# Moving the output bias into accumulating DMAs, and three halving adds for a reduction, in a fused attention and MLP kernel

## The chip, the cores and the metric

The kernel runs on one core of a Trainium2 chip. The metric is the device time of one execution in microseconds (us), taken as the median of several executions. The kernel before takes 215.47 us (three executions, 214.64 to 215.5). The profile is one of these executions; its span, from the first instruction to the last, is 212.9 us.

The engines are named as the profile names them: PE is TensorE (matmuls), PEld its weight loads, DVE is VectorE, ACT is ScalarE, POOL is GpSimd, SP is SyncE, which here only issues DMAs.

## What is computed

A layer norm of x feeds two branches, and both are added to x. With S = 2048 rows of D = 640:

```python
xn = layernorm(x)                          # rows of 640
q, k, v = split(xn @ wqkv)                 # 32 heads of 20
# row s attends to the 8 rows s, s-2, ..., s-14; rows before 0 get -1e9
logits[h, s, w] = (q[h, s] . k[h, s - 2*w]) * 20**-0.5
attn = softmax(logits, axis=w)
o[h, s] = sum_w attn[h, s, w] * v[h, s - 2*w]
out = x + o @ wo + (gelu(xn @ w1 + b1) @ w2 + b2)      # w1: 640 x 1536
```

All inputs and the output are bfloat16.

## The kernel before

The rows are worked in four chunks of 512 (`CH`), each with four blocks of 128. A small list scheduler inside the program fixes the order of instructions on PE, DVE, ACT and SP: each piece has an engine, an estimated duration, a rank, the pieces it needs and the buffers it holds. A table of rank offsets (`RANK`) tunes that order. The engines then run their instructions in this fixed order and wait on semaphores. POOL is outside of this order.

The pieces that matter here, for chunk n:

```python
# buffers: name, how many
("acc", 4), ("L", 1), ("O", 1), ("xnT", 3), ..., ("prod", 4),
("e", 1), ("attn", 1), ("ax", 1), ("oT", 1), ("hT", 18), ("osb", 2), ...

def do_ld():                                  # SP, after the transposes of chunk 1
    nc.sync.dma_start(w2_sb[:], ...)
    nc.sync.dma_start(wo2[:], ...)
    nc.sync.dma_start(b2bc[:], b2_bcast)      # b2 on all 128 partitions

def do_xb(n):                                 # DVE: x + b2, then stored to the output rows
    cs = slice(n * BPC, (n + 1) * BPC)
    nc.vector.tensor_tensor(out=x_sb[:, cs, :], in0=x_sb[:, cs, :],
        in1=b2bc[:].unsqueeze(1).to_broadcast([P, BPC, D]), op=ALU.add)
    cs = slice(n * BPC, min((n + 1) * BPC, LASTB))
    nc.sync.dma_start(out_sd.rearrange("(b p) d -> p b d", p=P)[:, cs, :], x_sb[:, cs, :])

def do_qk(n, wp, i):                          # DVE: q * shifted k, 128 x 2560 (two per wp)
    nc.vector.tensor_tensor(out=prod[:, i, :, :], in0=q, in1=k[:, :, off : off + CH], op=ALU.mult)

def logits(L, prod, wp):                      # PE: sums over a head's channels, into PSUM tile L
    for t in range(KT):
        for j in range(BPC):
            nc.tensor.matmul(L[j * H : (j + 1) * H, 2 * wp : 2 * wp + 2, :], lhsT=head_of[:],
                             rhs=prod[:, :, t, j * P : (j + 1) * P], ...)

# softmax over the 8 positions w, tile [128, 8, 128]
def do_mask():                                # chunk 0 only, DVE on PSUM
    nc.vector.tensor_tensor(out=L[0:H, :, 0:MW], in0=L[0:H, :, 0:MW], in1=mask[:], op=ALU.add)
def do_max(n): nc.vector.tensor_reduce(...)   # m over w
def do_sub(n): nc.vector.tensor_tensor(...)   # z = L - m
def do_exp(n): nc.scalar.activation(e[:], tiles["z", n][:], ACT.Exp, scale=SCALE)
def do_sum(n):
    nc.vector.tensor_reduce(out=ssum[:], in_=e.rearrange("p w c -> p c w"), axis=AX.X, op=ALU.add)
def do_recip(n): nc.vector.reciprocal(rs[:], tiles["ss", n][:])
def do_attn(n): nc.vector.tensor_tensor(...)  # e * rs

# attn is broadcast to the channels of each head by DMA (SP and ACT queues) into ax,
# DVE multiplies shifted v with it (do_av, 8 per chunk, 128 x 2560 each), adds the eight
# in pairs (do_add, do_add, do_add, then do_ot, which writes oT)

def do_f1(n, ft): ...                         # PE: 5 matmuls of 512 columns -> hps (PSUM, "acc")
def do_ge(n, ft): ...                         # ACT: gelu -> hT
def do_pj(n, which, to): ...                  # PE: 5 matmuls of 512 columns -> pps; chunks 1 to 3
                                              # (chunk 0 uses 128 columns each: gps)
def do_o(n, bl, pc, parts):                   # PE: one output block, 5 parts: 12 pairs from hT, w2
    ...                                       # and 5 pairs from oT, wo (the last part)
    nc.tensor.matmul(lo[:], lhsT=lhs, rhs=rhs[:, 0:CH], ...)
    nc.tensor.matmul(hi[:, 0 : D - CH], lhsT=lhs, rhs=rhs[:, CH:D], ...)
def do_oc(n, bl):                             # ACT: PSUM -> osb
    nc.scalar.copy(osb[:, 0:CH], lo); nc.scalar.copy(osb[:, CH:D], hi)
def do_od(n, bl):                             # POOL's queue: osb is added to the output rows
    nc.gpsimd.dma_start(rows, osb[:], accum_op=ALU.add)
```

For chunks 0 to 2 each output block uses one pair of PSUM tiles (`lo`, `hi`, the buffer "O"), so a block can start only when ACT has copied the block before it out. The last block of all is not accumulated by DMA: VectorE adds `x_sb` to its PSUM tiles and stores them (`do_oclo`, `do_ochi`).

Of the kernel before, what the change touches and what calls it, by code (L numbers as in the profile page):

```python
# [11 lines left out]
ALU = mybir.AluOpType  # L12
AX = mybir.AxisListType
BF16 = mybir.dt.bfloat16
F32 = mybir.dt.float32
PE, VE, SE, DQ = "pe", "ve", "se", "dq"


class Plan:
# [101 lines left out]
S, D, F, H, W, DIL = 2048, 640, 1536, 32, 8, 2  # L121
P = 128
# [3 lines left out]
CH = 512  # L126
NCH = S // CH
BPC = CH // P
# [3 lines left out]
MASKED = -1e9  # L132
MW = 16
LASTB = S // P - 1
# [4 lines left out]


RANK = {
    "ad02": 77, "av2": -4.2, "f11": 11.8, "f12": 26.1, "ge0": 15.4, "gj1": -111.8, "gj2": -25.5, "o00": -38,
    "o10": 29.1, "o11": 22.3, "o12": 28, "o13": 9.4, "o20": 9.6, "o21": 2.7, "o22": -7.9, "pj11": -100.5,
    "qk3": -49.5, "rc1": -43.4, "rc3": -86.1, "st2": 49.8, "st3": 51.7, "xn2": 23.8,
}


def make_plan(fns, offsets=RANK):

    pl = Plan(offsets)  # L150
# [6 lines left out]
    def f(kind, *a):  # L157
        return lambda: fns[kind](*a)
# [6 lines left out]
    for n in range(NCH):  # L165
        base = n * PERIOD
        prev = base - PERIOD
        early = base + (-37.0 if n == 1 else -85.0)
        xnT, q, k, v, oT = (("xnT", n), ("q", n), ("k", n), ("v", n), ("oT", n))
# [11 lines left out]
        for bl in range(BPC):  # L181
            xn, tp = ("xn", n, bl), ("acc", "tp", n, bl)
# [5 lines left out]
            pl.add(f"tc{n}{bl}", SE, 0.65, early + -3.0 if n else -99, [f"tp{n}{bl}"], f("tc", n, bl), [tp, xnT])  # L188
        if n == 1:
            pl.add("ld", DQ, 9.2, -1000, [f"tc1{bl}" for bl in range(BPC)], f("ld"))  # L190
        pl.add(f"xb{n}", VE, 1.43, base + 36, [f"xn{n}{bl}" for bl in range(BPC)] + ["ld"], f("xb", n))

        if n == 0:
            for bl in range(BPC):
                for g, parts in enumerate(GROUPS):
                    ps, last = ("acc", "g", bl, g), max(p[0] for p in parts)
# [5 lines left out]
        for which, buf in enumerate((q, k, v)):  # L202
# [5 lines left out]
            if which:  # L208
                need = done(n - 1, which) if n else []
                bufs = [buf] + ([("k" if which == 1 else "v", n - 1)] if n else [])  # L210
                pl.add(f"pad{n}{which}", SE, 0.26, early if n else -50, need, f("pad", n, which), bufs)

        L = ("L", n)
        for wp in range(W // 2):
            pr = ("prod", "qk", n, wp)
            for i in range(2):
                need = done(n, 0) + done(n, 1) + [f"pad{n}1"]
                pl.add(f"qk{n}{wp}{i}", VE, 1.42, base + 3.0 * wp + i, need, f("qk", n, wp, i), [q, k, pr])
            group = 2 if n else 4
            if wp % group == group - 1:  # L220
                wps = range(wp - group + 1, wp + 1)
                need = [f"qk{n}{x}{i}" for x in wps for i in range(2)] + ([f"lg{n}{wp-group}"] if wp > group else [])
                every = [("prod", "qk", n, x) for x in wps]
                pl.add(f"lg{n}{wp}", PE, 0.16 + 0.52 * group, n - 1000, need, f("lg", n, wps), every + [L], slack=0.8)

        e, at, ax = ("e", n), ("attn", n), ("ax", n)
        m, rs, ss, z = ("m", n), ("rs", n), ("ss", n), ("prod", "z", n)
        if n == 0:
            pl.add("mk", VE, 0.26, n - 1000, ["lg03"], f("mask"), [L])
        pl.add(f"m{n}", VE, 1.22, n - 1000, [f"lg{n}3"] + ([] if n else ["mk"]), f("max", n), [L, m])  # L230
        pl.add(f"mx{n}", VE, 1.22, n - 1000, [f"m{n}"], f("sub", n), [L, m, z])
        pl.add(f"ex{n}", SE, 1.02, n - 1000, [f"mx{n}"], f("exp", n), [z, e], table="exp")
        pl.add(f"ss{n}", VE, 1.93, n - 1000, [f"ex{n}"], f("sum", n), [e, ss])
        pl.add(f"ri{n}", VE, 0.96, n - 1000, [f"ss{n}"], f("recip", n), [ss, rs])
        pl.add(f"at{n}", VE, 1.22, n - 1000, [f"ri{n}"], f("attn", n), [e, rs, at])
        pl.add(f"xs{n}", SE, 1.2, n - 1000, [f"at{n}"], f("xs", n), [at, ax])
# [3 lines left out]
        for wp in range(W // 2):  # L240
            for i in range(2):
                need = [f"xd{n}", f"xs{n}", f"pad{n}2"] + done(n, 2)
                pl.add(f"av{n}{wp}{i}", VE, 1.42, base + 15.0 + 6.0 * wp + i, need, f("av", n, wp, i), [v, ax, prs[wp]])
        for k2, (a, b, r) in enumerate(((0, 1, 9.0), (2, 3, 21.0), (0, 2, 22.0))):
            need = [f"av{n}{x}{i}" for x in (a, b) for i in range(2)] if k2 < 2 else [f"ad{n}0", f"ad{n}1"]
# [8 lines left out]
        for bl in range(BPC):  # L254
            ob = ("osb", n, bl)
            O = [("O", n, bl)] if n < NCH - 1 or bl % 2 == 0 else [("acc", "lo", n, bl), ("acc", "hi", n, bl)]
            final = n * BPC + bl == LASTB
            last = None
            for pc in range(5):
                need = [last] if last else [f"ge{n}{ft}" for ft in range(FT)] + [f"xb{n}", "ld"]  # L260
                if pc == 4:
                    need.append(f"ot{n}")
                us = (0.65, 0.65, 0.65, 0.65, 1.08)[pc] if final else (0.82, 0.82, 0.82, 0.82, 1.37)[pc]
                last = pl.add(f"o{n}{bl}{pc}", PE, us, base + PERIOD + 8.0 + 8.0 * bl, need, f("o", n, bl, pc, ("lo",) if final else ("lo", "hi")), O + (hTs if pc == 0 else hTs[3 * pc : 3 * pc + 3] if pc < 4 else [oT]))
            if final:
                pl.add("oclo", VE, 0.65, base, [last], f("oclo"), O + [ob])
                last = pl.add("ohi", PE, 1.05, base + PERIOD + 90, [last], f("ohi"), O)
                pl.add("ochi", VE, 0.25, base, [last], f("ochi"), O + [ob])
                continue
            pl.add(f"oc{n}{bl}", SE, 0.78, base, [last], f("oc", n, bl), O + [ob])  # L270
            pl.add(f"od{n}{bl}", SE, 0.0, base, [f"oc{n}{bl}"], f("od", n, bl), [ob])
# [4 lines left out]
def kernel(  # L276
# [16 lines left out]
    nc = tc.nc  # L293
# [3 lines left out]
    out_sd = out.rearrange("b s d -> (b s) d")  # L297
    x_nb = x_sd.rearrange("(b p) d -> p b d", p=P)

    consts = ctx.enter_context(tc.tile_pool(name="consts", bufs=1))  # L300
# [8 lines left out]
    smp = ctx.enter_context(tc.tile_pool(name="smp", bufs=1))  # L309
# [6 lines left out]
    x_sb = wts.tile([P, NCH * BPC, D], BF16, name="x_sb")  # L316
# [3 lines left out]
    wo2 = wts.tile([P, KT, D], BF16, name="wo2")  # L320
    b1_rt = consts.tile([P, P], BF16, name="b1_rt")
    b2bc = consts.tile([P, D], BF16, name="b2bc")
    wqkv_v = A_wqkv.rearrange("(t p) n -> p t n", p=P)
    b2_bcast = bass.AP(tensor=B_b2.tensor, offset=B_b2.offset, ap=[[0, P], [1, D]])
    nc.sync.dma_start(x_sb[:, 0, :], x_nb[:, 0, :])
# [6 lines left out]
    for n in range(1, NCH):  # L332
        cs = slice(n * BPC, (n + 1) * BPC)
# [13 lines left out]
    nc.gpsimd.memset(eps_t[:], EPS)  # L347
    warm = consts.tile([P, 1], F32, name="warm")
    nc.scalar.activation(warm[:], eps_t[:], ACT.Sqrt)
    mask = consts.tile([H, W, MW], F32, name="mask")  # L350
    nc.gpsimd.memset(mask[:], 0.0)
    for w in range(1, W):
        nc.gpsimd.memset(mask[:, w, 0 : DIL * w], MASKED)
    head_of = consts.tile([P, H], BF16, name="head_of")
    b1T = consts.tile([P, FT], F32, name="b1T")

# [75 lines left out]
            tiles["tp", n, bl][:, 0 : KT * P].rearrange("p (t m) -> p t m", t=KT),  # L432
        )


    def do_td(n, bl):
        xnT = get(("xnT", n), lambda: xtp.tile([P, KT, CH], BF16, tag="xnT", name="xnT"))
        nc.sync.dma_start_transpose(xnT[:, :, bl * P : (bl + 1) * P], tiles["xn", n, bl][:])

    def do_xb(n):  # L440
        cs = slice(n * BPC, (n + 1) * BPC)
        nc.vector.tensor_tensor(
            out=x_sb[:, cs, :],
            in0=x_sb[:, cs, :],
            in1=b2bc[:].unsqueeze(1).to_broadcast([P, BPC, D]),
            op=ALU.add,
        )
        cs = slice(n * BPC, min((n + 1) * BPC, LASTB))
        nc.sync.dma_start(out_sd.rearrange("(b p) d -> p b d", p=P)[:, cs, :], x_sb[:, cs, :])


    def qkv_tile(n, which):
# [66 lines left out]
            op=ALU.mult,  # L519
        )  # L520

    def do_lg(n, wps):
        L = get(("L", n), lambda: psL.tile([P, W, P], F32, tag="L", name="L"))
        for wp in wps:
            logits(L, tiles["qk", n, wp], wp)

    def do_mask():
        L = tiles["L", 0]
        nc.vector.tensor_tensor(out=L[0:H, :, 0:MW], in0=L[0:H, :, 0:MW], in1=mask[:], op=ALU.add)

    def logits(L, prod, wp):
        for t in range(KT):
            for j in range(BPC):
                nc.tensor.matmul(  # L534
                    L[j * H : (j + 1) * H, 2 * wp : 2 * wp + 2, :],
                    lhsT=head_of[:],
                    rhs=prod[:, :, t, j * P : (j + 1) * P],
                    start=(t == 0 and wp % 2 == 0),
                    stop=(t == KT - 1 and wp % 2 == 1),
                    skip_group_check=True,  # L540
                )
# [22 lines left out]
        nc.scalar.activation(e[:], tiles["z", n][:], ACT.Exp, scale=SCALE)  # L564

    def do_sum(n):
        ssum = smp.tile([P, P], F32, tag="ssum", name="ssum")
        tiles["ss", n] = ssum
        nc.vector.tensor_reduce(
            out=ssum[:], in_=tiles["e", n][:].rearrange("p w c -> p c w"), axis=AX.X, op=ALU.add  # L570
        )

    def do_recip(n):
        rs = smp.tile([P, P], F32, tag="rs", name="rs")
        tiles["rs", n] = rs
        nc.vector.reciprocal(rs[:], tiles["ss", n][:])

    def do_attn(n):
        attn = smp.tile([P, W, P], BF16, tag="attn", name="attn")
# [98 lines left out]
    def do_oclo():  # L678
        osb = outp.tile([P, D], BF16, tag="osb", name="osb")
        tiles["osb", last] = osb  # L680
        nc.vector.tensor_tensor(out=osb[:, 0:CH], in0=tiles["lo", *last][:], in1=x_sb[:, LASTB, 0:CH], op=ALU.add)  # L681
        nc.sync.dma_start(out_sd[LASTB * P :, 0:CH], osb[:, 0:CH])

    def do_ohi():
# [3 lines left out]
    def do_ochi():  # L688
        osb = tiles["osb", last]
        nc.vector.tensor_tensor(  # L690
            out=osb[:, CH:D], in0=tiles["hi", *last][:, 0 : D - CH], in1=x_sb[:, LASTB, CH:D], op=ALU.add
        )
        nc.scalar.dma_start(out_sd[LASTB * P :, CH:D], osb[:, CH:D])

# [39 lines left out]
```

## Time and profile before

| what | value |
|---|---|
| time, median of three | 215.47 us |
| span of the profiled execution | 212.9 us |
| PE busy | 206.3 us |
| DVE busy | 181.0 us |
| ACT busy | 106.9 us |
| POOL busy | 14.4 us |
| bias additions on DVE (L442, 128 x 2560) | 4 of 1485 ns |
| reductions for the sum on DVE (L569) | 4 of 1909 ns |
| mask addition on DVE (L529) | 1 of 287 ns |
| output stores on POOL (L673) | 15, median 3.4 us from issue to landing |
| x stores on SP (L449) | 4, 2.7 to 8.0 us from issue to landing |
| broadcasts ax<-attn | 16 issues of 256 KB, median some 6 us to landing |

The busy share of an engine counts its instructions only, and matmuls overlap one another, so a busy PE is read together with its list of waits. A row in the list of groups gives line, engine, operation, output and inputs with shapes, the count, the busy time, the mean duration in ns of one, and the idle time of the engine just ahead of it. The slices divide the span into 40 stretches of 5.3 us, and each digit is a busy share in tenths.

### The profile page before, as it was taken

The page shows a single profiled execution, that of the slowest core. Times are in us where ns is not written, and L with a number is a line of the kernel's source. Part 1 is how long each engine was busy: PE and PEld are TensorE (multiplying, and loading weights), DVE is VectorE, ACT ScalarE, POOL GpSimd, SP SyncE. Part 2 cuts the span into 40 slices and gives each one's busy share as a digit, 9 for nine tenths or more (in the row PEclk, how much of TensorE's full clock was granted, in tenths as well). Part 3 has the DMA queues.
Part 4 walks back from the last instruction along what each step waited for, and adds up shares of the span by engine and source line. Part 5 has one row for each costly group of instructions (what it writes and reads, how often), then busy time and mean ns, then how long its engine had stood idle before and what let it go on. Part 6 is the DMA issues. An engine that isn't in the chain of part 4 may idle for free.

```text
span 212.9 us, 3938 instructions
## 1 busy us (share of the span) xinstructions
PE 206.3 (97%) x1667; PEld 121.4 (57%) x1690; DVE 181.0 (85%) x171; ACT 106.9 (50%) x190; POOL 14.4 (7%) x32
## 2 busy tenths in 40 slices
PE   7899999999999999999999999999999999999994
PEld 7799845644644556556555555556454555555552
DVE  3849899699999999997999999999999869995001
ACT  3667895798469664725346462243565311351210
POOL 2000000000000000110001100110101011101220
PEclk9999999999999999999999999999999999999999
DMA  6999539556711210227002080220205912152223
GB/s 217 366 367 370 83 68 329 217 167 172 199 31 31 56 39 0 31 34 197 0 3 31 4 211 17 31 29 5 32 3 83 259 20 30 24 123 31 34 31 63
DMA packets 21449, 21.49 MB, mean 101 GB/s; under 512 B 9016, under 2 KB 18616, under 8 KB 21432
## 3 DMA queue, kind: packets, MB, share of 16 engines
q1 hardware_dynamic: 17832, 16.49, 25.9%
q0 software_dynamic: 2160, 2.46, 9.5%
q10 hardware_dynamic: 1440, 2.29, 4.5%
q8 instruction: 13, 0.21, 0.4%
q14 instruction: 4, 0.03, 0.1%
HBM read 10.00 MB, written 5.08 MB: 71 GB/s over the span
## 4 chain that ended last, share of the span: by engine, by line
PE 95%; DMA 1%; DVE 1%; issue 1%; ACT 0%
PE lo L660 27%; PE hps L629 24%; PE pps L465 23%; PE gps L482 8%; PE hi L662 8%; PE L L534 4%; DMA x_sb<-in_A_x_dram 1%; PE tp L426 0%; DVE stats L385 0%; DVE stats L386 0%; ACT xnT L430 0%; DVE xn L412 0%; DVE mv L387 0%; DVE osb L690 0%; PE b_tp L366 0%
## 5 line engine op out<-in xcount | busy, mean ns | idle before, releaser
L629 PE MATMUL hps<-xnT,w_sb 128*128 128x512 bf16 x235 | 54.1, 379 | 0.3
L660 PE MATMUL lo<-w_sb,hT 128*128 128x512 bf16 x185 | 52.2, 379 | 0.0
L607 DVE TENSOR_TENSOR pv<-vT,ax 128x2560 bf16<-128x2560 bf16 x32 | 46.0, 1485 | 3.8 <-DMA ax<-attn 3.8
L515 DVE TENSOR_TENSOR prod<-qT,kT 128x2560 bf16<-128x2560 bf16 x32 | 45.5, 1483 | 0.0
L662 PE MATMUL hi<-w_sb,hT 128*128 128x128 bf16 x192 | 40.3, 219 | 0.6 <-issue 0.3
L640 ACT ACTIVATE hT<-hps,b1T 128x512 bf16<-128x512 f32 x48 | 31.3, 687 | 16.8 <-PE hps L629 12.2
L629 PEld LDWEIGHTS <-w_sb 128*128 128x128 bf16 x240 | 22.9, 98 | 26.8 <-issue 0.3
L616 DVE TENSOR_TENSOR pv<-pv 128x5120 bf16<-128x5120 bf16 x12 | 33.9, 2824 | 0.3
L667 ACT CAST osb<-lo 128x512 bf16<-128x512 f32 x15 | 8.8, 585 | 45.8 <-PE hi L662 21.6
L660 PEld LDWEIGHTS <-hT 128*128 128x128 bf16 x192 | 18.7, 98 | 22.6 <-issue 0.4
L673 POOL DMA_DIRECT2D out_dram<-osb x15 | 13.1, 875 | 192.4 <-ACT osb L668 192.4
L660 PE MATMUL lo<-wo,oT 128*128 128x512 bf16 x76 | 22.3, 379 | 0.1
L662 PEld LDWEIGHTS <-hT 128*128 128x128 bf16 x192 | 18.4, 98 | 1.8
L465 PE MATMUL pps<-xnT,wk_sb 128*128 128x512 bf16 x72 | 16.9, 380 | 0.2
L662 PE MATMUL hi<-wo,oT 128*128 128x128 bf16 x80 | 16.9, 219 | 0.2
L465 PE MATMUL pps<-xnT,wv_sb 128*128 128x512 bf16 x73 | 16.8, 379 | 0.2 <-issue 0.2
L465 PE MATMUL pps<-xnT,wq_sb 128*128 128x512 bf16 x73 | 16.8, 379 | 0.1
L660 PEld LDWEIGHTS <-oT 128*128 128x128 bf16 x80 | 7.8, 98 | 9.4
L681 DVE TENSOR_TENSOR osb<-lo,x_sb 128x512 bf16<-128x512 f32 x1 | 0.7, 691 | 14.5 <-PE lo L660 14.5
L385 DVE BATCH_NORM_STATS2 stats<-x_sb 128x6 f32<-128x320 bf16 x16 | 7.3, 459 | 6.7 <-DMA x_sb<-in_A_x_dram 6.5
L500 ACT CAST kT<-pps 128x512 bf16<-128x512 f32 x15 | 8.8, 584 | 8.2 <-PE pps L465 8.2
L465 PEld LDWEIGHTS <-wk_sb 128*128 128x128 bf16 x75 | 8.6, 118 | 7.4 <-issue 0.4
(61 smaller groups left out, 211.5 us busy)
## 6 DMA issues: line engine op xcount, KB each, us to landing
w_sb<-in_B_w_dram SPq DMA_DIRECT2D x2, 1920.0 KB, 11.6
out_dram<-osb POOLq DMA_DIRECT2D x15, 160.0 KB, 3.4
ax<-attn SPq DMA_DIRECT2D x8, 256.0 KB, 6.0
ax<-attn ACTq DMA_DIRECT2D x8, 256.0 KB, 5.5
x_sb<-in_A_x_dram SPq DMA_DIRECT2D x3, 640.0 KB, 11.4
out_dram<-x_sb SPq DMA_DIRECT2D x3, 640.0 KB, 3.7
wq_sb<-in_A_wqkv_dram SPq DMA_DIRECT2D x1, 800.0 KB, 4.8
wk_sb<-in_A_wqkv_dram SPq DMA_DIRECT2D x1, 800.0 KB, 7.0
```

Of the source, the lines that this page charges most:

```text
L465: nc.tensor.matmul(ps[:], lhsT=wqkv_p[which][:, ti, to, :], rhs=xnT[:, ti, :], start=(ti == 0), stop=(ti == KT - 1),)
L482: nc.tensor.matmul(ps[:, i, :], lhsT=wqkv_p[which][:, ti, to, :], rhs=tiles["xnT", 0][:, ti, cs], start=(ti == 0), stop=(ti == KT - 1),)
L500: nc.scalar.copy(dest[:, to, off : off + CH], tiles["pps", n, which, to][:])
L515: nc.vector.tensor_tensor(out=prod[:, i, :, :], in0=qkv_tile(n, 0)[:], in1=qkv_tile(n, 1)[:, :, off : off + CH], op=ALU.mult,)
L607: nc.vector.tensor_tensor(out=pv[:, i, :, :].rearrange("p t (j c) -> p t j c", j=BPC), in0=qkv_tile(n, 2)[:, :, off : off + CH].rearrange( ...
L616: nc.vector.tensor_tensor(out=ta[:], in0=ta[:], in1=tb[:], op=ALU.add)
L629: nc.tensor.matmul(ps[:], lhsT=w1_sb[:, ti, ft * P : (ft + 1) * P], rhs=tiles["xnT", n][:, ti, :], start=(ti == 0), stop=(ti == KT - 1),)
L640: nc.scalar.activation(hT[:], tiles["hps", n, ft][:], ACT.Gelu_apprx_tanh, bias=b1T[:, ft : ft + 1], scale=1.0)
L660: nc.tensor.matmul(lo[:], lhsT=lhs, rhs=rhs[:, 0:CH], start=first, stop=last)
L662: nc.tensor.matmul(hi[:, 0 : D - CH], lhsT=lhs, rhs=rhs[:, CH:D], start=first, stop=last)
L667: nc.scalar.copy(osb[:, 0:CH], tiles["lo", n, bl][:])
L673: nc.gpsimd.dma_start(rows, tiles["osb", n, bl][:], accum_op=ALU.add)
```

## The change

Four things are changed together.

1. The output rows first get x by a plain DMA (`do_xp`, SP), and then the bias b2, from its tile that holds it on all partitions, by an accumulating DMA (`do_xb`, POOL's queue). VectorE no longer adds the bias to x, except for the last block (`do_xl`), which does not go through accumulating DMAs. This frees VectorE and takes the dependence of the x store on VectorE away.
2. The exponentials are summed in three halving adds (8 to 4, 4 to 2, 2 to 1 positions) instead of one strided reduction.
3. The first chunk's logits are made in two groups of 40 matmuls, as those of the other chunks were already, instead of one group of 80. The mask for the first 14 rows is added by a matmul of one partition into PSUM after each group, instead of by VectorE.
4. The rank offsets are new, so that pieces stand in another order on all engines. POOL's four bias DMAs stand ahead of all 15 output stores.

The diff, cut to its core:

```diff
 RANK = {
-    "ad02": 77, "av2": -4.2, "f11": 11.8, ...
+    "ad00": 78, "av0": 30, "av1": 231.2, "av2": 188.6, "f10": 41.2, ...
 }
-        pl.add(f"xb{n}", VE, 1.43, base + 36, [f"xn{n}{bl}" for bl in range(BPC)] + ["ld"], f("xb", n))
+        pl.add(f"xp{n}", DQ, 0.3, base + 30, ["ld"], f("xp", n))
+        pl.add(f"xb{n}", DQ, 0.0, base + 33, [f"xp{n}"], f("xb", n))
...
-            group = 2 if n else 4
-            if wp % group == group - 1:
...
+            if wp % 2:
...
-        if n == 0:
-            pl.add("mk", VE, 0.26, n - 1000, ["lg03"], f("mask"), [L])
...
-        pl.add(f"ss{n}", VE, 1.93, n - 1000, [f"ex{n}"], f("sum", n), [e, ss])
+        pl.add(f"ss{n}", VE, 1.4, n - 1000, [f"ex{n}"], f("sum", n), [e, ss])
...
+                pl.add("xl", VE, 0.42, base - 40, ["ld"], f("xl"))
...
+    def rows(n):
+        cs = slice(n * BPC, min((n + 1) * BPC, LASTB))
+        return cs, out_sd.rearrange("(b p) d -> p b d", p=P)[:, cs, :]
+
+    def do_xp(n):
+        cs, dst = rows(n)
+        nc.sync.dma_start(dst, x_sb[:, cs, :])
+
     def do_xb(n):
-        cs = slice(n * BPC, (n + 1) * BPC)
-        nc.vector.tensor_tensor(
-            out=x_sb[:, cs, :],
-            in0=x_sb[:, cs, :],
-            in1=b2bc[:].unsqueeze(1).to_broadcast([P, BPC, D]),
-            op=ALU.add,
-        )
-        cs = slice(n * BPC, min((n + 1) * BPC, LASTB))
-        nc.sync.dma_start(out_sd.rearrange("(b p) d -> p b d", p=P)[:, cs, :], x_sb[:, cs, :])
+        cs, dst = rows(n)
+        nc.gpsimd.dma_start(dst, b2bc[:].unsqueeze(1).to_broadcast([P, cs.stop - cs.start, D]), accum_op=ALU.add)
+
+    def do_xl():
+        nc.vector.tensor_tensor(out=xlast[:], in0=x_sb[:, LASTB, :], in1=b2bc[:], op=ALU.add)
...
-    def do_mask():
-        L = tiles["L", 0]
-        nc.vector.tensor_tensor(out=L[0:H, :, 0:MW], in0=L[0:H, :, 0:MW], in1=mask[:], op=ALU.add)
+        if n == 0:
+            g = slice(2 * wp - 2, 2 * wp + 2)
+            nc.tensor.matmul(L[0:H, g, 0:MW], lhsT=ones_r[:], rhs=maskrow[:, g, :],
+                             start=False, stop=False, skip_group_check=True)
...
     def do_sum(n):
-        ssum = smp.tile([P, P], F32, tag="ssum", name="ssum")
-        tiles["ss", n] = ssum
-        nc.vector.tensor_reduce(
-            out=ssum[:], in_=tiles["e", n][:].rearrange("p w c -> p c w"), axis=AX.X, op=ALU.add
-        )
+        a = smp.tile([P, W // 2, P], F32, tag="sums", name="sums")
+        tiles["ss", n] = a
+        e = tiles["e", n]
+        nc.vector.tensor_tensor(out=a[:], in0=e[:, 0 : W // 2, :], in1=e[:, W // 2 :, :], op=ALU.add)
+        for k in (2, 1):
+            nc.vector.tensor_tensor(out=a[:, 0:k, :], in0=a[:, 0:k, :], in1=a[:, k : 2 * k, :], op=ALU.add)
```

## The prediction

> **What bounds the kernel now.** I read the page from the top: busy shares, then the slices, then the chain.
>
> ```profile
> PE 206.3 (97%) x1667; PEld 121.4 (57%) x1690; DVE 181.0 (85%) x171; ACT 106.9 (50%) x190; POOL 14.4 (7%) x32
> PE   7899999999999999999999999999999999999994
> DVE  3849899699999999997999999999999869995001
> PE 95%; DMA 1%; DVE 1%; issue 1%; ACT 0%
> ```
>
> TensorE (PE) is busy in 97% of the span, only the first slice and the last are thin, and the chain of work that ended last runs 95% through it. VectorE (DVE) is the second engine, at 85%, but it is not on that chain. A 97% share can still hide many small gaps, so the waits, asked for TensorE alone, are the deciding view (what waited, on what, us in total, times, longest):
>
> ```profile
> PE idle L701 <- POOL ident masks.py:199: 1.5, 1, 1.5
> PE tp L426 <- DVE xn L412: 0.4, 1, 0.4
> PE hi L662 <- issue: 0.3, 2, 0.2
> PE gps L482 <- ACT xnT L430: 0.2, 1, 0.2
> PE pps L465 <- issue: 0.2, 1, 0.2
> ```
>
> The reader is to see that this is the whole list: 2.6 us, of which 2.1 lie before 7.6 us, where the first input and its normalisation set the pace. From 7.6 us, when the first projections start, to 210.1 us, when the last matmul ends, TensorE waits 0.5 us in all. The chain's pieces at the two ends are 7.58 (first gps) and 209.15 + 0.96 (last hi). After it come 0.3 us of VectorE and about 2.4 us until the last store lands at 212.9.
>
> So the kernel stands on a floor of TensorE work. VectorE time that is taken away cannot be turned into span: at most the 0.5 us of gaps is there to win, 0.2%. It could do harm, however, if a new wait stops TensorE, for nothing behind that engine has slack to give the time back.
>
> **What the Trainium skill says.** "VectorE: DVE Perf Modes", section "The perf-mode tier table", has tensor_reduce at the basic rate only, and tensor_tensor at twice that for bf16 in SBUF and at the basic rate for fp32. The trace agrees: the reduction of 1024 bf16 takes 1909 ns, a product of 2560 bf16 1485 ns, an fp32 subtraction of 1024 1224 ns. "DMA: Bandwidth & Descriptors", section "SWDGE vs HWDGE vs iDMA", says that accumulating DMAs go out from GpSimd alone, whose software writes the descriptors; here the 15 accumulating stores are all on POOL's queue, 865 ns each. "SBUF — State Buffer", section "Who interferes with whom", infers that tensor_tensor does not keep GpSimd from writing descriptors; the trace agrees, since 14 of the 15 issues take at most about 0.87 us while VectorE is over 80% busy.
>
> **The change, part by part.**
>
> *VectorE.* Removed: four bias additions of 2560 elements (row L442, 4 x 1485 ns = 5.9 us), the mask addition (0.29 us), four reductions (4 x 1.91 = 7.6 us). Added: the bias for the last block alone, 640 elements, a quarter of 1.48 us, 0.4 us. The halving adds have 512, 256 and 128 output elements. I size them by the rows with fp32 operands that have such sizes: 691 ns for 512 (L681), 292 ns for 128 (L690), and 0.43 us between them, so 1.41 us a chunk, 5.6 us in all. The sum is 6.0 - 13.8 = -7.8 us, VectorE to some 173 us. None of it lies on the chain: 0 us of span.
>
> *TensorE.* The first chunk's logits come in two pieces of 40 matmuls instead of one of 80, each followed by one mask matmul of 4 x 16 columns from one partition: about 0.1 us each by the 58 ns pitch of the 128-column matmuls in the first phase. Add 0.2 us. All other matmuls are the same, in another order.
>
> *Order.* The new ranks move pieces on every engine. The places where TensorE could now wait: (a) the first logits. The products start, after one more block of statistics than before, near 25.1 us; four at a pitch of 1.40 us end at 30.8, and TensorE comes to them at 32.9 (25.3 for the end of the start-up, plus 7 pieces of 5 matmuls at 1.08). Two us in hand. (b) The first chunk's attention output. Counting VectorE's new order on from 25.1 with the durations of the trace (16 products 22.3, two statistics 2.0 with a wait to 39.8 for the logits, softmax, 8 weighted products 11.4, three adds 8.3, the second softmax in between) oT ends near 86.8. TensorE wants it at 87.4: half a microsecond in hand. (c) The attention broadcast is no longer held up on SyncE's (SP's) queue by the x store waiting for a bias addition; VectorE had waited 2.5 us for it at 172. It gains slack that is not needed.
>
> *DMA and POOL.* Here lies the risk. Before, an x store carried the bias already. Now x is stored and then b2 is added by an accumulating DMA, four of them, 3 x 640 KB and 480 KB, all from POOL's queue, and POOL's order places all four ahead of the first output store. That store therefore waits for the last of them to be issued, and its data queue up behind theirs. The third and fourth x stores come on SP after the second chunk's broadcast and the last transpose.
>
> Times: the broadcast needs the buffer that the first chunk's weighted products release, about 77.2 us by the count in (b). Two issues took 2.4 us, a transpose 1.2, an x store 0.4, so the last three x stores go out at 81 to 82.5. A store of 384 rows landed in 2.7 us alone, others in 3.7 to 8.0, and these follow a broadcast that lands in 6: I put them at 86, 88 and 90. An output store of 128 rows costs POOL 0.87 us; 512 rows, if that scales, cost 3.5. So POOL issues the three at 86 to 89.5, 93 and 95.5, and the first output store at 95.5 to 96.5 instead of about 89.7, when its data are ready. Data: an output store lands in 3.4 us, 0.87 of it issue; the trace's packets of these stores take 0.12 to 0.18 us, 8 to an engine. Three bias stores have 32 + 32 + 24 packets per engine: 10.6 us at 0.12, 13 at 0.15. Starting at 88 to 90, they end at 98.5 to 103, and the first output store lands 1.5 us later, at 100 to 104.5.
>
> Who needs it: there are two osb buffers. The third copy (osb<-lo) can start only when the first output store has read its buffer. TensorE finishes that block at about 100.4: 25.3 + 51 pieces x 1.08 + 5 logit pieces x 1.21 + 3 output blocks x 4.64. It then does one logit piece (1.2 us) and wants the same PSUM pair for the next block, which needs the copy's end (0.86 us later). So the wait turned into TensorE time is the landing minus some 100.6: 0 in the early case, 4 in the late one. The later bias work is over by then, and the other output stores are 5 to 15 us apart.
>
> **Sum.** 215.5 - 0 (VectorE) + 0.2 (matmuls) + about 0.7 (buffer wait, weighted towards none because each figure above was taken on the cautious side) = 216.4.
>
> **The rivals.** *Nothing shows*: TensorE stays full, VectorE idles more, 214.8 to 215.9. For it: the waits of TensorE above, and that the first output store had 10 us between its readiness and the need for its buffer. *The accumulating DMAs become the bound in one place*: TensorE stops near 101 us, 217 to 220. For it: POOL's order and the 4 times larger issues; against it: descriptors may be written faster for large transfers than four times 0.87. *VectorE was the bound after all*: a gain of up to 7.8 us, 208. Against it: VectorE is not on the chain and TensorE lists no wait on it after 7 us. *The new order starves the start*: loads of w2 and b2 are issued after the fourth transpose, later than before by some 2 us, and the last-block addition waits for b2 ahead of the first softmax. If b2 lands after 44.4 us, (b) loses its half microsecond and up to 1 us is paid at 87.
>
> **Range and chances.** The floor and the spread of the kernel before (214.64 to 215.5) give 214.8 as the low end; the full buffer wait plus some of (b) gives 220.0. Faster by over 2% would need 4.3 us from an engine with 0.5 us of waits: 0.02. Slower by over 2% needs the late case of the DMA chain: 0.15. The rest, 0.83, is within 2%.
>
> **What would show it.** VectorE's busy time near 173 us, with three short adds a chunk in place of 1.9 us. TensorE's waits: still none on VectorE. POOL: four larger issues, and the first output store issued after 95 us. If the copy osb<-lo shows a wait on a DMA near 100 us and TensorE one on that copy just after, the second rival is right; if TensorE stands near 87 us on oT, point (b) is. The prediction is wrong if TensorE's gaps lie anywhere else, if accumulating DMAs with 512 rows are much slower than their packets suggest, or if matmuls run at another pitch in the new order.

## The result, and the profile after

The changed kernel takes 216.51 us (six executions, 216.28 to 217.53), the kernel before 215.13 us beside it (six, 214.64 to 215.5). The ratio of the mean times is 1.0073, with a 95% interval of 1.0049 to 1.0098: slower by 0.7%, some 1.4 us between the medians, although VectorE has less to do. (All times here are medians, and all ratios are of means.)

The page of the changed kernel: busy times, the slices of TensorE and VectorE, and the chain's shares by engine.

```profile
PE 206.2 (96%) x1668; PEld 121.0 (56%) x1692; DVE 173.7 (81%) x175; ACT 109.5 (51%) x192; POOL 19.6 (9%) x37
PE   7799999999999999999799999999999999999994
DVE  3859999569999999999999999999997999602001
PE 85%; DMA 9%; DVE 1%; issue 1%; POOL 1%; ACT 1%; SPq 1%; ACTq 0%
```

VectorE is down by 7.3 us. TensorE's busy time is the same, but its row of slices has a 7 in the middle, at slice 20, from 101.8 to 107.2 us. The chain, which was 95% TensorE, now runs 9% of the span through DMAs. TensorE's waits name the event (what waited, on what, us in total, times, longest):

```profile
PE idle L715 <- POOL ident masks.py:199: 1.6, 1, 1.6
PE lo L674 <- ACT osb L681: 1.3, 1, 1.3
PE tp L428 <- DVE xn L414: 0.9, 1, 0.9
PE gps L488 <- ACT xnT L432: 0.2, 1, 0.2
PE hi L676 <- issue: 0.2, 1, 0.2
```

The second line is new: one matmul into `lo` waited 1.3 us for an output copy of ScalarE. What that copy waited for is in ScalarE's waits:

```profile
ACT osb L681 <- DMA out_dram<-osb: 7.0, 1, 7.0
```

And the chain between 82 and 104 us tells the rest, read from top to bottom (start us, us, what):

```profile
82.59 1.53 SPq L448
84.12 0.05 issue
84.17 5.34 DMA out_dram<-x_sb
89.51 0.28 issue
89.80 1.99 POOL out_dram L452 x2
91.78 11.00 DMA out_dram<-osb
...
102.88 0.59 ACT osb L681
103.48 0.04 issue
103.52 0.38 PE lo L674
```

The x stores of the later chunks go out on SyncE's queue. When one has landed, POOL issues the last two bias DMAs and then the first output store, and that store takes 11.0 us to land. In the kernel before, the median of these stores was 3.4 us, and the slowest took 6.9. ScalarE's third output copy, which needs the buffer of that store, starts at 102.88, and TensorE resumes at 103.52.

### The profile page after: what moved, and what is told of

Its sections match the earlier page's. It is cut to its first block, busy times and chain, and to the rows that moved or that the text cites. A ratio compares the mean times of both kernels' runs of the same rounds, so it can differ in the third digit from the quotient of the medians.

```text
span 214.4 us, 3948 instructions
## 1 busy us (share of the span) xinstructions
PE 206.2 (96%) x1668; PEld 121.0 (56%) x1692; DVE 173.7 (81%) x175; ACT 109.5 (51%) x192; POOL 19.6 (9%) x37
## 4 chain that ended last, share of the span: by engine, by line
PE 85%; DMA 9%; DVE 1%; issue 1%; POOL 1%; ACT 1%; SPq 1%; ACTq 0%
PE hps L643 23%; PE lo L674 23%; PE pps L471 21%; PE gps L488 8%; PE hi L676 7%; DMA out_dram<-osb 5%; PE L L547 3%; DMA out_dram<-x_sb 2%; DMA x_sb<-in_A_x_dram 1%; POOL out_dram L452 1%; SPq L448 1%; PE tp L428 0%; DVE stats L387 0%; DVE stats L388 0%; ACT xnT L432 0%
## 5 line engine op out<-in xcount | busy, mean ns | idle before, releaser
L695 DVE TENSOR_TENSOR osb<-lo,xlast 128x512 bf16<-128x512 f32 x1 | 0.7, 691 | 16.1 <-PE lo L674 16.1
L452 POOL DMA_DIRECT2D out_dram<-b2bc x4 | 5.3, 1337 | 85.1 <-DMA out_dram<-x_sb 85.1
L471 PEld LDWEIGHTS <-wv_sb 128*128 128x128 bf16 x75 | 8.7, 117 | 7.3
```

The source lines that it names most:

```text
L452: nc.gpsimd.dma_start(dst, b2bc[:].unsqueeze(1).to_broadcast([P, cs.stop - cs.start, D]), accum_op=ALU.add)
L471: nc.tensor.matmul(ps[:], lhsT=wqkv_p[which][:, ti, to, :], rhs=xnT[:, ti, :], start=(ti == 0), stop=(ti == KT - 1),)
```

## The experiments

All were run on the chip against the kernel before. The theory (A) was the buffer wait: accumulating bias DMAs delay the first output store, it holds one of two `osb` buffers, and TensorE stops for want of the copy. The rivals were (B) the new order or the mask matmuls and (C) the load of the DMAs as such. Two more runs asked whether VectorE's time was worth anything.

### Three output buffers

```diff
-    outp = ctx.enter_context(tc.tile_pool(name="outp", bufs=2))
+    outp = ctx.enter_context(tc.tile_pool(name="outp", bufs=3))
```

The room comes from keeping the maximum and the reciprocal inside the tile of the sums; the order on each engine is that of the changed kernel.

> The changed kernel with three osb buffers in place of two (room for the third comes from keeping the maximum and the reciprocal in the tile of the sums); the same bias DMAs and the same order on every engine. Theory A, the buffer wait (the third output copy waits until the first output store, whose data stand behind three bias DMAs, has left its buffer): ScalarE's wait of 7.0 us on the output store goes, TensorE's gap of 1.3 us goes, 215.2 us. Theory B, the loss lies in the new order or in the mask matmuls: 216.5 us as the changed kernel. Theory C, the DMA load itself slows the engines or their transfers: 216.5 us.

Measured: 215.34 us, ratio to before 0.9994 (0.9977 to 1.0011). The first output store is as late as it was, as POOL's rows in the timeline show (start us, us, line, operation, [idle before <- releaser]):

```profile
91.30 2.58 POOL L452 DMA_DIRECT2D out_dram<-b2bc  x2 [0.38 <-DMA out_dram<-x_sb]
93.37 1.45 POOL L688 DMA_DIRECT2D out_dram<-osb  x1
```

The slowest of its output stores takes 10.9 us to land. But nobody waits for it, as ScalarE's third copy in its timeline shows:

```profile
102.40 0.59 ACT L682 CAST osb<-lo 128x512 bf16<-128x512 f32 x1 [5.18 <-PE lo L675]
```

It waits for TensorE's matmul again, not for a DMA, and TensorE has no wait on a copy any more. The profiled execution itself was the slowest of 15, 216.71 us, with 1.2 us of waits for the projection weights before 11.1 us. So B and C fall: with the same order, the same mask matmuls and the same DMAs, one more buffer gives the whole loss back.

### The bias DMAs left out

```diff
     def do_xb(n):
         cs, dst = rows(n)
-        nc.gpsimd.dma_start(dst, b2bc[:]...to_broadcast(...), accum_op=ALU.add)
+        pass
```

The bias is then missing from the output, except in the last block.

> The changed kernel without the four accumulating bias DMAs; the bias is left out of the output, save in the last block. Theory A: the first output store lands 3.4 us after its data are ready near 90, no wait on a buffer, 215.2 us. Theory B: 216.5 us. Theory C: 215.2 us, and faster than the kernel with three buffers.

Measured: 215.28 us, ratio 1.0004 (0.9988 to 1.002). POOL issues the first output store when its data are ready, at 90.7 us, and no output copy waits for a DMA. The third copy starts at 101.25 us, in place of 102.88:

```profile
101.25 0.59 ACT L681 CAST osb<-lo 128x512 bf16<-128x512 f32 x1 [5.22 <-issue]
```

The time is not below that of the kernel with three buffers, so beyond the buffer wait these DMAs cost nothing that is measured.

### The bias DMAs of chunks 1 to 3 issued later

```diff
-        pl.add(f"xb{n}", DQ, 0.0, base + 33, [f"xp{n}"], f("xb", n))
+        pl.add(f"xb{n}", DQ, 0.0, base + 33, [f"xp{n}"], f("xb", n), after=112.0 if n else 0.0)
```

POOL is put under the fixed order too, so that this place holds.

> The changed kernel with the bias DMAs of chunks 1 to 3 placed on POOL's queue after the four output stores of chunk 0; the same DMAs, the same buffers, the same order elsewhere. Theory A: no wait of the third output copy, and the bias DMAs, some 12 us of data after 111 us, are done before chunk 1 has its first output store ready at 131; 215.2 us. Theory B: 216.5 us. Theory C: 216.5 us, with the loss moved to 111 to 125 us.

Measured: 215.69 us, ratio 1.0012 (0.9997 to 1.0027). POOL's timeline has the three bias DMAs after chunk 0's four output stores, and a wide gap before the next:

```profile
90.61 0.89 POOL L687 DMA_DIRECT2D out_dram<-osb  x1 [27.59 <-ACT osb L682]
96.29 0.86 POOL L687 DMA_DIRECT2D out_dram<-osb  x1 [4.79 <-ACT osb L682]
102.27 0.86 POOL L687 DMA_DIRECT2D out_dram<-osb  x1 [5.12 <-ACT osb L682]
108.43 0.86 POOL L687 DMA_DIRECT2D out_dram<-osb  x1 [5.31 <-ACT osb L682]
108.98 4.25 POOL L452 DMA_DIRECT2D out_dram<-b2bc  x3
130.08 0.91 POOL L687 DMA_DIRECT2D out_dram<-osb  x1 [16.86 <-ACT osb L682]
```

TensorE has no gap there, and the profiled span is 213.2 us, as without the bias DMAs (213.3). The same three transfers, moved by 20 us, cost the engines nothing, although they fill the DMA engines from 110 to 122 us. The time exceeds the span by 2.5 us here and by 2.1 elsewhere; why the part outside of the span is longer stays open.

### The bias DMAs as plain stores

```diff
-        nc.gpsimd.dma_start(dst, b2bc[:]...to_broadcast(...), accum_op=ALU.add)
+        nc.gpsimd.dma_start(dst, b2bc[:]...to_broadcast(...))
```

The rows then hold the bias without x, which is left out of the output save in the last block.

> The changed kernel with the bias DMAs as plain stores on the same queue (they overwrite x, so x is left out of the output, save in the last block): the same bytes, issues and order, no accumulation. Theory A with the accumulation rate as the cause (0.12 to 0.15 us a packet against 0.06 for a plain one): three bias stores take 5 to 6 us in place of some 12, the first output store lands near 97, no wait, 215.2 us. If it is the bytes, the issue on POOL or the wait for the x stores that delay the output store, 216.5 us and ScalarE's wait stays near 7 us.

Measured: 215.41 us, ratio 1.0005 (0.9991 to 1.0019). In the list of DMA issues (KB each, median us from issue to landing), first of the changed kernel, then of this one:

```profile
out_dram<-b2bc POOLq DMA_DIRECT2D x3, 640.0 KB, 7.5
out_dram<-b2bc POOLq DMA_DIRECT2D x1, 480.0 KB, 10.9
```

```profile
out_dram<-b2bc POOLq DMA_DIRECT2D x3, 640.0 KB, 4.3
out_dram<-b2bc POOLq DMA_DIRECT2D x1, 480.0 KB, 5.2
```

The bytes, the queue, the order and the place are the same, and the first output store is still issued at 92.0 us behind them. It now lands in 5.4 us at most, and ScalarE's third copy starts at 101.16 with no wait on a DMA:

```profile
101.16 0.59 ACT L681 CAST osb<-lo 128x512 bf16<-128x512 f32 x1 [5.22 <-PE hi L676]
```

One thing changed with the accumulation: the packets, the pieces in which the profile records a transfer. POOL's queue in the changed kernel and in this one (packets, MB, share of the time of 16 engines):

```profile
q0 software_dynamic: 4144, 4.92, 17.0%
q0 software_dynamic: 2704, 4.92, 12.9%
```

The four bias stores went out as 1920 packets of 1280 bytes when they accumulated, and as 480 of 5120 bytes when they did not. The size of the packets does not explain the rate, however. A plain packet of 5120 bytes took 0.24 us in the mean, 0.06 for each 1280 bytes, and the plain x stores of the kernel before, in packets of 1280 bytes, took 0.06 us a packet as well. The accumulating packets of 1280 bytes took 0.13. So it is neither the issue on POOL nor the bytes that delay the store, but that these stores accumulate.

### Chunk 1's bias DMA twice

```diff
-        nc.gpsimd.dma_start(...)
+        for _ in range(2 if n == 1 else 1):
+            nc.gpsimd.dma_start(...)
```

Chunk 1's rows get the bias twice. POOL is under the fixed order here too.

> The changed kernel with chunk 1's bias DMA issued twice (its rows get the bias twice), so POOL holds one more DMA of 640 KB ahead of the first output store; the second waits for the first to land. Theory A, dose and response: chunk 1's first lands near 95, its second, and chunks 2 and 3 after it, have 32 + 32 + 24 packets per engine at about 0.135 us from 97 us on, so the first output store lands near 111 in place of 102.8; ScalarE's wait grows by 8 us, TensorE's gap from 1.3 to about 9, 224.5 us. If the buffer wait is only a companion of the loss, the time stays within 1 us of the changed kernel's.

Measured: 225.45 us over two executions, ratio 1.0476 (1.043 to 1.0522). The two waits grow together: ScalarE's copy on the store from 7.0 to 13.6 us, TensorE on the copy from 1.3 to 7.9 us.

```profile
ACT osb L682 <- DMA out_dram<-osb: 13.6, 1, 13.6
...
PE lo L675 <- ACT osb L682: 7.9, 1, 7.9
```

The dose has its response: of the 8.4 us by which the profiled span is longer than the changed kernel's (222.8 against 214.4), 6.6 are TensorE's longer wait. Another part, which the expectation did not have, is seen in the stretches after it (us; busy time and count for PE, PEld, DVE, ACT and POOL; granted clock; DMA share; GB/s):

```profile
102.00:110.00 8.00, 0.51 (x20) 0.32 (x12) 7.70 (x5) 0.27 (x1) 0.00 (x0) 0.79 1.13 185
110.00:112.00 2.00, 1.63 (x7) 0.80 (x7) 0.00 (x0) 1.97 (x4) 0.86 (x1) 0.50 0.00 1
112.00:114.00 2.00, 2.00 (x12) 0.93 (x10) 0.00 (x0) 1.98 (x4) 0.00 (x0) 0.65 0.78 85
114.00:116.00 2.00, 2.00 (x17) 1.17 (x16) 0.00 (x0) 1.99 (x2) 0.00 (x0) 1.00 0.04 5
```

TensorE comes back from the wait at half its clock. Until 113.5 us its pairs of matmuls follow each other at 0.54 us instead of 0.27, which costs some 1.6 us more.

### VectorE's time alone

Two runs took VectorE's work out of the kernel before, in its own order. The first has only the three halving adds in place of the reduction:

> The kernel before with the three halving adds alone in place of the reduction; the order on every engine as before. If VectorE has slack, VectorE's busy time falls by 4 x 0.5 = 2.0 us and the time does not move: 215.3 us. If VectorE were the bound in part, up to 2 us less.

Measured: 214.97 us, ratio 0.9994 (0.9975 to 1.0013). The second leaves VectorE's four bias additions out, and with them the bias:

```diff
     def do_xb(n):
-        cs = slice(n * BPC, (n + 1) * BPC)
-        nc.vector.tensor_tensor(out=x_sb[:, cs, :], in0=x_sb[:, cs, :], in1=b2bc..., op=ALU.add)
         cs = slice(n * BPC, min((n + 1) * BPC, LASTB))
         nc.sync.dma_start(...)
```

> The kernel before without VectorE's four bias additions (the bias is left out of the output); the order as before. If VectorE has slack, its busy time falls by 5.9 us and the time does not move: 215.3 us. If VectorE were the bound, up to 5.9 us less, near 209.5.

Measured: 215.3 us, ratio 0.9999 (0.9981 to 1.0016). Their busy times, in this order:

```profile
PE 208.2 (98%) x1690; PEld 121.7 (57%) x1690; DVE 179.0 (84%) x179; ACT 107.0 (50%) x190; POOL 14.4 (7%) x32
```

```profile
PE 208.0 (97%) x1690; PEld 121.3 (57%) x1690; DVE 175.5 (82%) x167; ACT 106.4 (50%) x190; POOL 14.4 (7%) x32
```

VectorE falls from 181.0 to 179.0 and to 175.5 us, and the time stays within 0.2%. (TensorE's 206.3 us before are of 1667 recorded matmuls, against 1690 here, so its busy times are not compared.) The rival that VectorE was the bound, at up to 7.8 us, is gone.

## Why the prediction was right, point by point

**The bound.** That TensorE's list of waits decides, and that VectorE's time cannot become span, held: with some 7.3 us less on VectorE, the four repaired kernels take 215.28 to 215.69 us, where the kernel before took 215.33 beside them. None is lower by more than the noise.

**VectorE's sizes.** The halving adds were put at 1.41 us a chunk. The groups by form give 686 + 425 + 291 ns = 1.40:

```profile
L583 DVE TENSOR_TENSOR sums<-e 128x512 f32<-128x512 bf16 x4 | 2.7, 686 | 0.5 <-ACT e L577 0.5
...
L585 DVE TENSOR_TENSOR sums<-sums 128x256 f32<-128x256 f32 x4 | 1.7, 425 | 0.1
L585 DVE TENSOR_TENSOR sums<-sums 128x128 f32<-128x128 f32 x4 | 1.2, 291 | 0.1
```

From 128 to 256 elements the time grows by 134 ns and from there to 512 by 261, 1.02 to 1.05 ns an element (the largest add reads bf16 and writes fp32). That fits what the Trainium skill's "VectorE: DVE Perf Modes" says in "The perf-mode tier table", the basic rate for fp32 (2293 ns for 2048 elements there). So the adds gain 0.5 us a chunk without a faster mode.

One reading in the prediction does not hold: that the trace shows the reduction at the basic rate. Two reductions, of the kernel before and of the changed one:

```profile
L569 DVE TENSOR_REDUCE ssum<-e 128x128 f32<-128x1024 bf16 x4 | 7.6, 1909 | 0.2 <-ACT e L564 0.2
L560 DVE TENSOR_REDUCE m<-L 128x128 f32<-128x1024 f32 x4 | 4.9, 1221 | 2.4 <-PE L L535 2.2 <-PE L L547 0.2
```

The reduction for the maximum takes 1221 ns for 1024 elements, like the fp32 subtraction of as many (1224). The one for the sum takes 1909, in the same order over the positions, so it ran slower than that. Against a reduction of 1221 ns the three adds, at 1402, would have lost; they gain because this one is slow. Why it is slow is not shown: the two reductions differ in the type and the memory of what they read, and in the operation.

**Point (a), the first logits.** TensorE came to them at 32.80 us (32.9 predicted) and did not wait. The mask matmuls cost about 0.1 us each: the next matmul starts 0.12 and 0.13 us after them.

**Point (b), the first oT.** It ended at 87.43 us instead of 86.8, and TensorE used it at 87.89: the half microsecond held. b2 landed late, as the last rival said, and VectorE waited 1.5 us for it, but after its small addition it still waited 0.5 us for the exponential, so b2 delayed nothing.

**The DMA chain.** The outcome was right, its parts partly wrong. The x stores were issued at 82.6 to 86.1 us rather than 81 to 82.5, because the last transpose ahead of them took 3.75 us on SyncE and not 1.2, and the three issues 4.0 us and not 3 x 0.4. POOL's issue of 512 rows was put at 3.5 us by four times 0.87; it took 1.3. So the first output store was issued at 91.8 us and not after 95: the term "if that scales" failed. It did not matter, because the data, not the issue, set the landing. They were put at 10.6 to 13 us from 88 to 90 on; in the trace the packets of the three bias stores and the first two output stores run from 90.1 to 103.3 us, 0.132 us each in the mean. The store landed at 102.8 us, inside the range of 100 to 104.5.

**The rivals.** The sign that the prediction named for its second rival came true, a copy `osb<-lo` that waits on a DMA near 100 us and TensorE on that copy just after. The mechanism is that rival's, which the sum had weighed at 0.7 us, and its size is below the rival's range of 217 to 220 us. "Nothing shows", 214.8 to 215.9, did not come.

**The size of the wait.** TensorE stood 1.27 us where the weighted guess was 0.7. The prediction's own rule, the landing minus 100.6, gives 2.2 us at the measured landing. That is 0.9 too much, mostly because TensorE finished the third block at 101.0 us and not at 100.4; it also resumed 0.74 us after the landing, where the rule counted 0.86 for the copy alone. The sum came to 216.4 us against 216.51 measured, and that closeness is luck: the three executions of before that the prediction started from gave 215.47 us, 0.3 above the 215.13 measured beside the change, and this made up for part of the wait that was set too small.

## What to carry to other kernels

When one engine has nearly no waits in its own list, time taken from another engine is not worth having, as the 7.3 us of VectorE were not here, and each relief has to be read for what it puts in the way. Work moved to DMAs that accumulate sits in the same queue as the stores behind it: count the packets ahead of the first store that somebody needs the buffer of. Here a third buffer, or a later place on the queue, took the harm away without taking the work away.

## What the runs showed of the hardware beyond expectation

An accumulating store of 640 KB in 1280-byte rows took 7.5 us from issue to landing, a plain one from the same queue and place 4.3; a packet of 1280 bytes took 0.132 us in the mean, against 0.06 for the plain x stores of the kernel before. Issuing 512 rows from POOL took 1.3 us in the changed kernel where 128 took 0.86, so most of the cost did not grow with the rows. With the three bias DMAs in a row behind an output store, in the run that issued them later, one took up to 2.7 us; as plain stores they took 0.75 to 0.93.

TensorE's clock fell to half after a wait of 7.9 us and came back some 3 us later, but did not fall after one of 1.3 us: the changed kernel's granted clock is 1.00 from 102 to 108 us. The Trainium skill's "TensorE: Matmul & The Clock Gate", section "What's actually happening", has the same two states, half clock after an idle window of about 3.4 us and full clock after as long a busy one; here a wait of 7.9 us halves the clock, one of 1.3 us does not, and the full rate is back 3.1 us after the matmuls resume.
